# Two block products by seven: the second matrix of an MLP for two token blocks, with its weights' sums made late, and an identity matrix made on another engine

## The chip, the cores and the metric

The kernel runs on one NeuronCore of a Trainium2 chip. The core has TensorE (matrix products into PSUM), VectorE (DVE), ScalarE (ACT) and GpSimd (POOL) for elementwise work, and SyncE (SP), which here issues all DMAs from a single queue in program order. The metric is the time on the device of one execution in microseconds (us); lower is better. 0.2% of it is about what a measurement can tell.

## The reference

Three parts follow each other: an attention without a score matrix, and two MLPs. All tensors are float32 except the weights, which are float64.

```python
# q, k, v: (8 batches, 8 heads, 576, 64)
q_s = softmax(q, axis=-1);  k_s = softmax(k, axis=2)
kv = einsum('bhsd,bhse->bhde', k_s, v)
x = einsum('bhsd,bhde->bhse', q_s, kv)          # -> (4608 tokens, 512)
h = x @ w_in                                    # 512 -> 2048, the first MLP
g = maximum(h, 0) ** 2
x2 = g @ w_out                                  # 2048 -> 512: the matrix of this change
out = (sigmoid(x2 @ w_gate) * (x2 @ w_val)) @ w_out2   # 512 -> 1536 -> 512
```

## The kernel before

**Tiles and precision.** The 4608 tokens are nine blocks of 512 (numbers 0 to 8). Every float32 operand of a product is split into a rounded part hi and the rest lo, and `mm3` issues three matmuls for one product: hi hi, hi lo, lo hi (lines 217 to 219, which is why these three lines carry nearly all of TensorE's time). `hi_of` (ACT, line 211) rounds, `lo_of` (VectorE, line 214) subtracts.

**Seven products.** Most large products are 2 x 2 block products done by Strassen's seven products (`PRODUCTS`, in the order 1, 5, 6, 2, 7, 3, 4) instead of eight. The data side of it is `plan_b`: sums `b_comb` (line 715) and splits `b_hi`, `b_lo` of four quarters. The result side is `plan_seven`: three pairs of PSUM banks, with copies `e_copy` and additions `e_add` (line 777) between products. The weight side is `plan_w`: a weight group of four tiles (float64 words turned to float32 by `w_abs`, `w_low`, `w_bits`, `w_round`) is combined (`w_comb`, line 292) and split, and each hi/lo pair is stored to DRAM by `w_store` (line 296) and fetched again for every use by `w_fetch` (line 301). For the kind "out", w_out, `plan_w` stores just the four plain quarters 1, 2, 0, 4 of each group and stops.

**Stages.** Blocks 0 and 1 go through `conv_stage` while the weights are prepared. The others go in pairs (2,3), (4,5), (6,7) and the single 8 through `in_stage` (the first MLP) and `gate_stage` (the second). The order is in_stage 1, in_stage 2, gate_stage 0, gate_stage 1, in_stage 3, in_stage 4, gate_stage 2, 3, 4; the attention of later blocks runs beside them. An `in_stage` does two halves h. A half first makes 1024 columns of h and g in two units of seven products (`plan_in`), then multiplies by w_out with `o_mm`: plain 2 x 2 blocks, for two token halves tq, four kk, two output halves oh, 12 matmuls each. `o_ev` evacuates: for h = 0 a copy, stored to DRAM as "xp" (line 924); for h = 1 "xp" is loaded again (`o_ld`, line 917), added to the bank (line 913) and stored as "x2".

**Order.** All of this is added to a `Plan` with a due time and the engines' assumed durations. `Plan.trace` simulates the engines once, when the program is built: each engine takes the ready operation with the smallest due time for which buffers are free. The order so found is the program order of each engine on the chip. Buffers that matter here (`SIZES`): "W" 10 (weight tiles of 0.5 MB, fetched or to be stored), "S" 6 (split data of the second matrix), "a" 6 (results to be stored), "w" 5 (float32 weight tiles; some gate results also lie in them). Weight fetches are chained in their order of use.

**Start.** Before the plan, line 1249 calls `make_identity`: GpSimd clears `ident` and runs an affine select on it (masks.py lines 197, 199). VectorE copies `ident` with swapped columns into `swap` (line 1253), GpSimd fills `ones`, `kv` and `vt`. `ident` is used for TensorE's transposes (`k_turn`, line 404; `q_turn_pe`) and `k_put`. The first attention steps are `k_max` (lines 396 to 399), `k_turn`, and `k_mm`, the product of k^T and v (line 445).

Of the kernel before, what the change touches and what calls it, by code (L numbers as in the profile page):

```python
# [10 lines left out]
F32 = mybir.dt.float32  # L11
# [5 lines left out]
ALU = mybir.AluOpType  # L17
# [9 lines left out]
CHOSEN = object()  # L27
# [110 lines left out]
PRODUCTS = (1, 5, 6, 2, 7, 3, 4)  # L138
# [5 lines left out]
def attention_mlp_mlp(  # L144
# [159 lines left out]
    def plan_w(kind, g, T, dT, tag, conv, lead=6.0):  # L304
# [50 lines left out]
        split(3, 1, t1 + 6 * s, [M("S4")], give=[tag])  # L355
        add(t1 + 7 * s, {FREE: 0.0}, ("wfree", kind, g), lambda: None, after=[O(5), O(6), O(3)], give=[tag] * 2)


# [446 lines left out]

    def plan_seven(uid, t, nb, n, pe, tags):

# [9 lines left out]
        for i in PRODUCTS:  # L817
# [5 lines left out]
            if copy:  # L823
                for b in range(nb):
                    add(t, {ACT: ua}, E(copy, b), e_copy, uid, copy, pr, b, n, tags[copy][b], after=[names[b]], take=[tags[copy][b]])
                last[pr] = [E(copy, b) for b in range(nb)]
            elif adds:
                for b in range(nb):
                    add(t, {DVE: uv}, E(adds + "+", b), e_add, uid, adds, pr, b, n, after=[names[b], E(adds, b)])
                last[pr] = [E(adds + "+", b) for b in range(nb)]  # L830
                end[adds] = [E(adds + "+", b) for b in range(nb)]
            else:
                end["p4"] = names
# [58 lines left out]
    def o_mm(uses, gn, tq, oh, kk, pr, n):  # L892

        for m in range(2):
            ps = banks[pr[m]][:, 0:n]
            for r in range(2):
# [3 lines left out]
                mm3(ps, w[:, 0, c:c + 128], w[:, 1, c:c + 128], x[:, 0], x[:, 1], kk == 0 and r == 0, kk == 3 and r == 1)  # L900

    def o_ev(key, bank, h, n, engine):
        src = banks[bank][:, 0:n]
# [11 lines left out]
    def o_ld(key, c):  # L915
        t = tile2("a", "xp")[:, c]
        nc.sync.dma_start(out=t, in_=x2d["xp", key[0], key[1]][:, c])
        z_t[key] = t

    def o_st(key, h, c):  # L920
# [153 lines left out]
    BLOCKS = [(2 * n, 2 * n + 1) for n in range(NPAIR)] + [(NB - 1,)]  # L1074

    def in_stage(n, t):

# [4 lines left out]
        for h in range(2):  # L1082
            G = ("G", n, h)
            gready = defaultdict(dict)
            for u in range(2):
# [10 lines left out]
                freed[prs[0]] = (t, fin)  # L1096

            for kk in range(4):
                for qn, (name, where) in gready[kk].items():
# [138 lines left out]
    for i, (stage, n) in enumerate(STAGES):  # L1238
# [3 lines left out]
        if stage is gate_stage and n == 0:  # L1242
            preps = [("gv", g) for g in range(gv_n)] + [("out2", g) for g in range(out2_n)]
            for m, (kind, g) in enumerate(preps):
                plan_w(kind, g, T1 - 40 + (t + 40 - T1 + 40) / len(preps) * m, 10.0, "w", None)
        t = stage(n, t)

    ctx.enter_context(tc.manual_schedule())
    make_identity(nc, ident)
    nc.gpsimd.memset(ones, 1.0)  # L1250
# [73 lines left out]
```

## Time and profile before

| | us |
|---|---|
| three timed runs | 1709.07, 1710.23, 1712.56 |
| median | 1710.23 |
| the profiled execution | 1712.01 |
| its span, first to last instruction | 1709.9 |
| TensorE busy in the span | 1645.8 (96%) |
| VectorE busy | 1123.3 (66%) |
| ACT busy | 921.4 (54%) |
| GpSimd busy | 20.7 (1%) |
| DMA, share of its 16 engines' time | 74% |

Busy time counts overlapping instructions of one engine once. Matmuls overlap each other in the trace (each is shown for about 0.39 us, and one starts every 0.227 us), so a stretch in which TensorE's busy time equals its length is one in which matmuls follow each other without a gap. The span is what the program itself takes; some 2 us lie around it.

### The profile page before, as it was taken

What the parts mean: (1) busy time and instruction counts of PE and PEld (TensorE: products, weight loads), DVE (VectorE), ACT (ScalarE), POOL (GpSimd) and SP (SyncE); (2) the same over time, 40 slices, a digit from 0 to 9 for tenths busy, and PEclk for the clock granted to TensorE, in tenths of its full rate; (3) what the DMA queues carried; (4) which work ended last, traced back from release to release, by engine and by line L of the source; (5) the groups of instructions that cost most, each with busy time, mean ns of one, the idle gap of its engine ahead of it and who ended that gap; (6) DMA issues with size and microseconds to landing.
All of it is one profiled execution on the core that took longest, in us unless ns stands there. A gap on an engine that the chain in (4) does not pass through costs nothing.

```text
span 1709.9 us, 25346 instructions
## 1 busy us (share of the span) xinstructions
PE 1645.8 (96%) x9276; PEld 1412.5 (83%) x9276; DVE 1123.3 (66%) x2078; ACT 921.4 (54%) x1718; POOL 20.7 (1%) x43
## 2 busy tenths in 40 slices
PE   4898999999899999999999999999999999999999
PEld 2676777877777888889888998889998899889998
DVE  6889768888865687588366874353364594448446
ACT  5688657758463655366355645263443453335344
POOL 0000000000000000000000000000000000000000
PEclk9899999999999999999999999999999999999999
DMA  7778888888697979976766573557777567555797
GB/s 257 268 281 320 320 316 308 309 288 313 210 349 259 357 260 370 334 255 206 242 214 197 194 236 121 210 185 285 283 285 242 191 204 239 194 195 185 239 379 269
DMA packets 163484, 443.30 MB, mean 259 GB/s; under 512 B 15648, under 2 KB 45856, under 8 KB 163360
## 3 DMA queue, kind: packets, MB, share of 16 engines
q1 hardware_dynamic: 163360, 441.68, 74.0%
q8 instruction: 74, 1.21, 0.3%
q14 instruction: 50, 0.41, 0.1%
HBM read 357.20 MB, written 84.41 MB: 258 GB/s over the span
## 4 chain that ended last, share of the span: by engine, by line
PE 81%; DVE 7%; DMA 6%; ACT 4%; issue 2%; SPq 0%; POOL 0%; DVEq 0%; POOLq 0%; ACTq 0%
PE bank L217 26%; PE bank L218 26%; PE bank L219 26%; DMA w_gv<-whl 2%; PE xps L595 2%; DMA wraw<-in_moe_w_gate_dram 1%; DVE whl L214 1%; DMA ws<-w_in 1%; DVE bX L214 1%; PE kps L452 1%; DVE wf L271 1%; DVE wf L278 1%; DMA wraw<-in_moe_w_out_dram 0%; DVE wf L268 0%; ACT whl L211 0%
## 5 line engine op out<-in xcount | busy, mean ns | idle before, releaser
L217 PE MATMUL bank<-bX,ws 128*128 128x512 f32 (+1 forms) x1288 | 476.3, 370 | 7.6 <-DMA ws<-w_in 5.9
L219 PE MATMUL bank<-bX,ws 128*128 128x512 f32 (+1 forms) x1288 | 472.2, 367 | 0.0
L218 PE MATMUL bank<-bX,ws 128*128 128x512 f32 (+1 forms) x1288 | 472.2, 367 | 0.0
L777 DVE TENSOR_TENSOR s<-s,bank 128x512 f32<-128x512 f32 (+1 forms) x303 | 189.8, 633 | 221.7 <-PE bank L219 177.1
L217 PEld LDWEIGHTS bank<-bX,ws 128*128 128x128 f32 x1288 | 243.5, 189 | 48.3 <-DMA ws<-w_in 6.3
L211 ACT ACTIVATE s<-bank 128x512 f32<-128x512 f32 (+1 forms) x303 | 164.4, 553 | 212.9 <-PE bank L219 195.8
L219 PEld LDWEIGHTS bank<-bX,ws 128*128 128x128 f32 x1288 | 243.2, 189 | 40.0
L218 PEld LDWEIGHTS bank<-bX,ws 128*128 128x128 f32 x1288 | 243.5, 189 | 37.9 <-issue 0.2
L211 ACT ACTIVATE bS<-s 128x512 fp32r<-128x512 f32 (+1 forms) x306 | 175.6, 582 | 156.5 <-PE bank L219 145.3
L214 DVE TENSOR_TENSOR bS<-s,bS 128x512 fp32r<-128x512 f32 (+1 forms) x306 | 190.6, 632 | 77.4 <-ACT bS L211 72.5
L217 PE MATMUL bank<-ws,bS 128*128 128x256 f32 x756 | 214.4, 284 | 0.0
L219 PE MATMUL bank<-ws,bS 128*128 128x256 f32 x756 | 214.0, 283 | 0.0
L218 PE MATMUL bank<-ws,bS 128*128 128x256 f32 x756 | 213.9, 283 | 0.0
L217 PE MATMUL bank<-bS,ws 128*128 128x512 f32 (+1 forms) x512 | 187.9, 367 | 4.3 <-DMA ws<-w_out 3.2
L218 PE MATMUL bank<-bS,ws 128*128 128x512 f32 (+1 forms) x512 | 186.4, 364 | 0.0
L219 PE MATMUL bank<-bS,ws 128*128 128x512 f32 (+1 forms) x512 | 186.3, 364 | 0.0
L217 PEld LDWEIGHTS bank<-ws,bS 128*128 128x128 f32 x756 | 145.0, 192 | 1.0
L218 PEld LDWEIGHTS bank<-ws,bS 128*128 128x128 f32 x756 | 145.0, 192 | 0.7
L796 ACT ACTIVATE s<-s 128x512 f32<-128x512 f32 (+1 forms) x120 | 70.4, 589 | 139.1 <-DVE s L777 138.6
L219 PEld LDWEIGHTS bank<-ws,bS 128*128 128x128 f32 x756 | 145.0, 192 | 0.0
L217 PEld LDWEIGHTS bank<-bS,ws 128*128 128x128 f32 x512 | 97.1, 190 | 20.7 <-DMA ws<-w_out 3.6
L219 PEld LDWEIGHTS bank<-bS,ws 128*128 128x128 f32 x512 | 97.1, 190 | 15.3
(128 smaller groups left out, 2131.4 us busy)
## 6 DMA issues: line engine op xcount, KB each, us to landing
ws<-w_gv SPq DMA_DIRECT2D x210, 512.0 KB, 4.4
ws<-w_out SPq DMA_DIRECT2D x185, 512.0 KB, 4.4
ws<-w_in SPq DMA_DIRECT2D x128, 512.0 KB, 6.0
w_gv<-whl SPq DMA_DIRECT2D x42, 512.0 KB, 5.2
w_out<-whl SPq DMA_DIRECT2D x37, 512.0 KB, 4.9
w_in<-whl SPq DMA_DIRECT2D x32, 512.0 KB, 4.1
wraw<-in_moe_w_out_dram SPq DMA_DIRECT2D x28, 512.0 KB, 5.5
vt<-in_v_dram SPq DMA_DIRECT2D x32, 325.0 KB, 5.9
```

What stands on the lines that cost most here:

```text
L211: nc.scalar.activation(out=dst, in_=src, func=AF.Copy)
L214: by_name[engine].tensor_tensor(out=dst, in0=src, in1=hi.bitcast(F32), op=ALU.subtract)
L217: nc.tensor.matmul(ps, ah, bh, start=first, stop=False, skip_group_check=True)
L218: nc.tensor.matmul(ps, ah, bl, start=False, stop=False, skip_group_check=True)
L219: nc.tensor.matmul(ps, al, bh, start=False, stop=last, skip_group_check=True)
L271: nc.vector.scalar_tensor_tensor(out=w, in0=high, scalar=-0x40000000, in1=w, op0=ALU.bitwise_and, op1=ALU.bitwise_or)
L278: by_name[engine].tensor_tensor(out=w, in0=w, in1=low, op=ALU.add)
L452: nc.tensor.matmul(ps[rows, o:o + D + 1], kt[:, r, rows], vt[:, r, c:c + D + 1], start=(r == 0), stop=(r == RK - 1), skip_group_check=True,)
L595: nc.tensor.matmul(ps[:, e], kvf[b % 2][p], t[:, e], start=True, stop=True)
L777: nc.vector.tensor_tensor(out=t, in0=t, in1=banks[pr[b]][:, 0:n], op=ALU.add)
L796: nc.scalar.activation(out=t, in_=t, func=AF.Sigmoid)
```

## The change

The second matrix of the first MLP is done by seven products for blocks 6 and 7 (`SEVEN`, both halves of `in_stage` 3). `seven_out` takes the place of the plain loop there: `plan_b` forms and splits the sums of g, `p_o1` issues 6 matmuls for each of the seven products, each kk and each of two banks, `plan_seven` evacuates. For h = 1 the copies become additions to the "xp" tile that was loaded (`e_old`). `o_st1` stores.

Seven products need the weights' four sums. `plan_out_sums` makes them, for each of the four groups: it loads the four stored pairs again (`w_again`), adds hi and lo to a whole tile (`w_whole`), forms S1 to S4 (`w_comb`), splits and stores them as products 5, 7, 6, 3. It is due around the end of the first gate stage, the groups 16 us apart, each after the one before.

The identity is made by VectorE: a row of column numbers by doubling, its transpose in blocks of 32, and a comparison for each of the four blocks on the diagonal. The fills of `ones`, `kv` and `vt` stay on GpSimd.

```diff
+    def w_again(g, b, i):
+        t = tile4("W", "wa")
+        nc.sync.dma_start(out=t.bitcast(F32), in_=wd["out", g, i])
+        wraw["out", g, b] = t
+    def w_whole(g, b):
+        t, hl = tile2("w", "wf"), wraw.pop(("out", g, b)).bitcast(F32)
+        nc.vector.tensor_tensor(out=t, in0=hl[:, 0], in1=hl[:, 1], op=ALU.add)
+        wf["out", g, b] = t
+    def plan_out_sums(g, T, dT, wait):
+        V = lambda b: ("vs", g, b)
+        M = lambda nm: ("wm", "out", g, nm)
+        O = lambda i: ("wo", "out", g, i)
+        for b, i in enumerate((1, 2, 0, 4)):
+            add(T + b * dT - 6, {DMA: 1.5}, ("vl", g, b), w_again, g, b, i, after=[("ws", "out", g, i), *wait], take=["W"])
+            add(T + b * dT, VEC, V(b), w_whole, g, b, after=[("vl", g, b)], take=["w"], give=["W"])
+        T += 4 * dT
+        for nm, o, a, b, op, after, i in (
+            ("S1", 3, 2, 3, ALU.add, [V(2), V(3)], 5), ("S3", 2, 0, 2, ALU.subtract, [V(0), M("S1")], 7),
+            ("S2", 0, 3, 0, ALU.subtract, [M("S3"), M("S1")], 6), ("S4", 1, 1, 0, ALU.subtract, [M("S2"), V(1)], 3),
+        ):
+            key = ("out", g, i)
+            add(T, VEC, M(nm), w_comb, "out", g, o, a, b, op, CHOSEN, after=after)
+            add(T + 0.2, {ACT: 0.63}, ("wh",) + key, w_hi, key, o, "W", after=[M(nm)], take=["W"])
+            add(T + 0.4, LOW, ("wo",) + key, w_lo, key, o, CHOSEN, after=[("wh",) + key])
+            add(T - 10, {DMA: 1.5}, ("ws",) + key, w_store, key, after=[O(i)], give=["W"])
+            T += dT
+        add(T, {FREE: 0.0}, ("wfree", "out", g, 1), lambda: None, after=[O(5), O(7), M("S2"), O(6), O(3)], give=["w"] * 4)
...
+    def e_old(uid, nm, pr, b, n, key):
+        t = z_t.pop(key)
+        nc.vector.tensor_tensor(out=t, in0=t, in1=banks[pr[b]][:, 0:n], op=ALU.add)
+        ev[uid, nm, b] = t
...
+                    if old:
+                        key = old(copy, b)
+                        add(t, {DVE: uv}, E(copy, b), e_old, uid, copy, pr, b, n, key, after=[names[b], ("old",) + key])
+                        continue
...
+    def p_o1(use, gn, i, kk, pr, n):
+        w = whl[use]
+        x = bs[gn + (kk,), i]
+        for m in range(2):
+            c = 256 * (kk % 2) + 128 * m
+            mm3(banks[pr[m]][:, 0:n], w[:, 0, c:c + 128], w[:, 1, c:c + 128], x[:, 0], x[:, 1], i in OPENS and kk == 0, kk == 3)
...
+    def o_st1(where, key, h, c):
+        z_t[key] = ev.pop(where)
+        o_st(key, h, c)
...
+    SEVEN = {(3, 0), (3, 1)}
+    def seven_out(n, h, t, js, nt, mm, G, gready):
+        per = 24 * mm * SLOW
+        for kk in range(4):
+            nm = G + (kk,)
+            for qn, (name, where) in gready[kk].items():
+                def bind(nm=nm, qn=qn, where=where):
+                    bq.setdefault(nm, {})[qn] = ev.pop(where)
+                add(t - 8, {FREE: 0.0}, ("bind", nm, qn), bind, after=[name])
+            times = {i: t + per * x + per / 4 * kk - 6 for x, i in enumerate(PRODUCTS)}
+            quarters = ("11", "12", "21", "22")
+            plan_b(nm, {qn: [("bind", nm, qn)] for qn in quarters}, times, "S", nt, {qn: ["f"] for qn in quarters})
+        sorder.extend([("bhi", G + (kk,), i) for i in PRODUCTS for kk in range(4)])
+        uid = ("o1", n, h)
+        def place(nm, b):
+            oh, tq = {"s1": (0, 0), "s2": (0, 1), "s5": (1, 1), "p4": (1, 0)}[nm]
+            if len(js) > 1:
+                return (js[tq], 2 * oh + b), slice(0, N)
+            return (js[0], 2 * oh + b, tq), slice(nt * tq, nt * tq + nt)
+        names = (("s1", 1), ("s5", 5), ("s2", 6), ("p4", 4))
+        if h:
+            for nm, i in names:
+                for b in range(2):
+                    key, c = place(nm, b)
+                    add(
+                        t + per * PRODUCTS.index(i) - 6, {DMA: 0.8}, ("old",) + key, o_ld, key, c,
+                        after=[("ost",) + key[:2] + (0,) + key[2:], ("blo", G + (0,), i)], take=["a"],
+                    )
+        def pe(i, pr, t, wait):
+            for kk in range(4):
+                use = (uid, i, kk // 2)
+                if kk % 2 == 0:
+                    plan_fetch(("out", 2 * h + kk // 2, i), use, t - 14)
+                nm = ("p", uid, i, kk)
+                add(
+                    t, {PE: 6 * mm}, nm, p_o1, use, G, i, kk, pr, nt,
+                    after=[("wf", use), ("blo", G + (kk,), i)] + (wait if kk == 0 else [("p", uid, i, kk - 1)]),
+                    give=["S"] + (["W"] if kk % 2 else []),
+                )
+                t += 6 * mm * SLOW
+            return [nm] * 2, t
+        end, prs, t = plan_seven(
+            uid, t, 2, nt, pe, {x: ["a", "a"] for x in ("s1", "s5", "s2")}, (lambda nm, b: place(nm, b)[0]) if h else None
+        )
+        fin = []
+        for b in range(2):
+            e = ("e", uid, "p4", b)
+            if h:
+                key = place("p4", b)[0]
+                add(t, {DVE: 0.7}, e, e_old, uid, "p4", prs[0], b, nt, key, after=[end["p4"][b], ("old",) + key])
+            else:
+                add(t, {ACT: 0.6, DVE: 0.7}, e, z_copy, uid, prs[0], b, nt, "a", CHOSEN, after=[end["p4"][b]], take=["a"])
+            fin.append(e)
+            for nm, _ in names:
+                key, c = place(nm, b)
+                last = e if nm == "p4" else end[nm][b]
+                add(t - 4, {DMA: 0.8}, ("ost",) + key[:2] + (h,) + key[2:], o_st1, (uid, nm, b), key, h, c, after=[last], give=["a"])
+        freed[prs[0]] = (t, fin)
+        return t
...
+            if (n, h) in SEVEN:
+                t = seven_out(n, h, t, js, nt, mm, G, gready)
+                continue
...
+            for g in range(NU):
+                wait = [("wfree", "out", g - 1, 1)] if g else [("wfree",) + x for x in preps]
+                plan_out_sums(g, t + D2_ - 10 + 16 * g, 2.0, wait)
...
-    make_identity(nc, ident)
+    col, row = (cst.tile([128, 32], F32, name=x) for x in ("colnum", "rownum"))
+    nc.vector.memset(col[:, 0:1], 0.0)
+    nc.vector.memset(col[:, 1:2], 1.0)
+    for n in (2, 4, 8, 16):
+        nc.vector.tensor_scalar(out=col[:, n:2 * n], in0=col[:, 0:n], scalar1=float(n), scalar2=None, op0=ALU.add)
+    nc.vector.memset(ident, 0.0)
+    nc.vector.transpose(out=row, in_=col)
+    for i in range(4):
+        c = slice(32 * i, 32 * i + 32)
+        nc.vector.tensor_tensor(out=ident[c, c], in0=row[c], in1=col[c], op=ALU.is_equal)
```

## Rows read from the trace of the kernel before

**Rows 1.** The page: busy us, share of the span and instructions of each engine.

```profile
PE 1645.8 (96%) x9276; PEld 1412.5 (83%) x9276; DVE 1123.3 (66%) x2078; ACT 921.4 (54%) x1718; POOL 20.7 (1%) x43
```

**Rows 2.** Busy time by stretch: us, each engine's (instructions), PEclk granted, DMA share, GB/s.

```profile
25.00:150.00 125.00, 103.09 (x454) 76.83 (x454) 112.90 (x236) 99.51 (x213) 0.00 (x0) 0.88 0.82 299
...
330.00:660.00 330.00, 316.40 (x1460) 258.62 (x1458) 240.21 (x428) 194.61 (x348) 3.82 (x5) 0.98 0.83 295
660.00:795.00 135.00, 134.78 (x751) 117.67 (x752) 98.67 (x162) 70.75 (x117) 1.41 (x2) 1.00 0.82 289
795.00:875.00 80.00, 80.00 (x486) 69.95 (x485) 43.95 (x79) 37.00 (x60) 2.41 (x3) 1.00 0.71 230
...
947.00:1013.00 66.00, 66.00 (x536) 64.06 (x535) 59.66 (x101) 38.59 (x66) 0.00 (x0) 1.00 0.65 206
...
1049.00:1094.50 45.50, 45.50 (x200) 37.03 (x199) 12.94 (x22) 11.71 (x20) 0.00 (x0) 1.00 0.27 94
1094.50:1134.70 40.20, 40.20 (x177) 32.69 (x176) 23.72 (x45) 26.43 (x48) 0.00 (x0) 1.00 0.73 259
1134.70:1178.30 43.60, 43.60 (x194) 36.08 (x194) 16.11 (x30) 10.88 (x23) 0.00 (x0) 1.00 0.51 177
1178.30:1198.40 20.10, 20.10 (x169) 20.10 (x168) 9.29 (x24) 12.79 (x35) 0.00 (x0) 1.00 1.00 389
```

**Rows 3.** Who TensorE waited for, whole span: total us, times, longest.

```profile
PE bank L404 <- DVE kmx L399: 14.5, 2, 12.6
...
PE bank L217 <- DMA ws<-w_in: 5.9, 1, 5.9
...
PE bank L217 <- DMA ws<-w_out: 3.2, 1, 3.2
...
PE bank L217 <- DMA ws<-w_gv: 0.7, 1, 0.7
```

**Rows 4.** Busy time of instructions on tile bS alone, second matrix of h = 1.

```profile
1134.80:1178.20 43.40, 43.40 (x192) 35.80 (x191) 7.50 (x11) 6.94 (x11) 1.00 0.51 176
```

**Rows 5.** Timeline of VectorE: start, us, what; two operations in a row.

```profile
170.69 1.29 DVE L292 TENSOR_TENSOR wf<-wf 128x512 f32<-128x512 f32 x2
```

**Rows 6.** Who the DMA queue waited for, whole span.

```profile
SPq L296 <- DVE whl L214: 140.6, 55, 7.3
```

**Rows 7.** Timeline of the start; then kt, vt, wraw: first and last issue, landing.

```profile
10.01 0.28 POOL masks.py:199 TENSOR_SCALAR_AFFINE_SELECT ident<-ident 128x128 f32<-128x128 f32 x1 [9.08 <-issue]
...
10.32 1.44 DVE L1253 COPY swap<-ident 128x64 f32<-128x64 f32 x2 [10.32 <-POOL ident masks.py:199]
...
10.53 1.23 DVE L396 TENSOR_TENSOR kmx<-kt 128x256 f32<-128x256 f32 x1
...
18.22 2.36 PE L445 MATMUL bank<-vt,kt 128*128 128x129 f32 x10
...
18.67 0.16 DVE L559 TENSOR_SCALAR qst<-qst 128x8 f32<-128x8 f32 x1
...
23.64 0.66 ACT L254 ACTIVATE wf<-wraw 128x512 f32<-128x512 f32 x1
...
L377 SPq DMA_DIRECT2D kt<-in_k_dram x1: 399/399/399, 0.7 to 0.7; - x1
...
DMA to landing us min/median/max: 3.1/3.1/3.1
...
L383 SPq DMA_DIRECT2D vt<-in_v_dram x1: 860/860/860, 4.9 to 4.9; - x1
...
DMA to landing us min/median/max: 6.5/6.5/6.5
...
L244 SPq DMA_DIRECT2D wraw<-in_moe_w_in_dram x2: 327/328/328, 8.5 to 9.1; - x2
...
DMA to landing us min/median/max: 6.6/6.9/7.2
```

**Rows 8.** The reductions on GpSimd: ns min/median/max, first and last start.

```profile
L422 POOL PARTITION_ALL_REDUCE kgm<-kmx x24: 704/705/1001, 161.3 to 922.1; - x24
```

More of the change, by code (lines that the diff above doesn't have):

```diff
@@ L8 @@
 from concourse._compat import with_exitstack
-from concourse.masks import make_identity
 F32 = mybir.dt.float32
@@ L804, in e_mul, with plan_seven @@
         by_name[engine].tensor_tensor(out=t, in0=t, in1=ev.pop((uid, o, b)), op=ALU.mult)
-    def plan_seven(uid, t, nb, n, pe, tags):
+    def e_old(uid, nm, pr, b, n, key):
+        t = z_t.pop(key)
+        nc.vector.tensor_tensor(out=t, in0=t, in1=banks[pr[b]][:, 0:n], op=ALU.add)
+        ev[uid, nm, b] = t
+    def plan_seven(uid, t, nb, n, pe, tags, old=None):
         order = sorted(pairs, key=lambda x: freed[x][0] if freed[x] else -1)
```

## The prediction

> **What bounds the kernel now.** I read the page's busy lines first: TensorE is busy for 1645.8 us of a span of 1709.9 us, so the other engines can only matter through it [rows 1]. Then the busy times by stretch, to see where the missing 64 us lie. The reader is to see two different kernels in that table [rows 2]. From 25 to 150 us TensorE works 103.1 of 125 us and VectorE 112.9: the prologue, a chain through VectorE. From 660 us on TensorE's busy time equals the stretch to within 0.2 us in every row, and VectorE's is anything from 36% to 90% of it: there the number of matmuls sets the time. The list of what TensorE waited for agrees [rows 3]: one wait of 12.6 us for VectorE's first maxima (14.5 us in two), and two for weight tiles (5.9 and 3.2 us). The change touches one thing in each of these two regimes, so I cost them apart.
>
> **Part 1, fewer matmuls in the second matrix of blocks 6 and 7.** Removed: each half h of that stage issues 2 tq x 4 kk x 2 oh x 12 = 192 matmuls of 128x512; the seven products need 7 x 4 x 6 = 168. For h = 1 the 192 took 43.40 us without a gap [rows 4], so 0.226 us each, and the clock is already at its upper level (1.00 granted, 2.4 GHz) [rows 2]. Two halves lose 48 matmuls: 48 x 0.226 = 10.85 us. As TensorE is continuous there, all of it counts, unless something that is added is late.
>
> **What is added beside these matmuls.** Each half now splits 28 operands where it split 16 (ACT rounds, VectorE subtracts), forms 16 differences on VectorE, and evacuates 14 banks where it evacuated 8. For h = 1 VectorE gains 12 + 16 + 6 = 34 operations. Two in a row take 1.29 us [rows 5], 0.69 for the first and 0.60 for each further one, so 34 take 20.5 us. VectorE was busy 16.1 of 43.6 us in that stretch [rows 2]; it would be 36.6 of 38.0 us, 96%. For h = 0 (12.9 us now) the same sum gives 33.4 us. The nearest stretch with products of this form ran VectorE at 59.7 of 66 us, 90%, and TensorE lost nothing [rows 2]; 96% is beyond it. What eases it: the stretches before and behind have VectorE at 23.7 of 40.2 and 9.3 of 20.1 us, and about 6 of 28 splits can run ahead into the six S buffers. What speaks against it: a product is 24 x 0.226 = 5.4 us, and its bank pair is wanted again two products later, so VectorE may run one product late and no more. Bounds: 0, and, if nothing at all could be shifted and each operation took its full 0.69 us, 16.1 + 34 x 0.69 - 38.0 = 1.6 us for h = 1, with as much again if the lateness recurs at the stage behind (block 8 waits for its own splits in the same VectorE queue). I take 1 us. ACT's 12 extra roundings per half (about 7 us) fit: ACT is busy 11 to 12 of 44 us in these stretches [rows 2]. The 12 extra fetches of weights (0.5 MB each) come where DMA moves 94 and 177 GB/s [rows 2], at one per 2.7 us, the rate at which the stretch 1094.5 to 1134.7 already fetches: nothing. The loads and stores of partial sums are as many as before.
>
> **The weights' sums.** For each of four groups: 4 loads of a stored hi/lo pair, 4 additions, 4 combinations, 4 ACT roundings, 4 subtractions, 4 stores. That is 48 VectorE operations, 48 x 0.60 = 29 us, 16 on ACT, and 32 transfers of 0.524 MB = 16.8 MB. The code makes them due at the start of the gate stage of blocks 2 and 3, near 800 us, and runs the groups one behind the other, 16 us apart. In 795 to 875 us VectorE is busy 43.95 of 80 us: with 29 more it is at 73, which the 90% stretch covers. DMA moves 230 GB/s there, 18.4 MB; with 16.8 more 440 GB/s would be wanted, more than the 389 GB/s of the busiest row [rows 2]. So the sums take longer than planned, about 35.2 / 0.389 = 90 us, which is harmless in itself: the first product that reads them is near 1055 us. It is not harmless that every load and store stands in SP's one queue. A store waits there for VectorE's subtraction (140.6 us of such waits in this trace, the longest 7.3 [rows 6]), and every weight fetch behind it waits too; so does one behind a load that waits for a free W buffer. The same mixture, the other weights being prepared, stands in 660 to 795 us, and TensorE lost 0.2 us of 135; in 330 to 660 us it stands beside two large waits for weights (5.9 and 3.2 us [rows 3]). Bounds: 0, and one wait of 5.9 us per group, 23.6 us. Nearest in kind (a gate stage, fetches of w_gv) is 660 to 795, so I take 1 us.
>
> **Part 2, the identity on VectorE.** Now GpSimd waits 9.08 us before its select, which ends at 10.3; VectorE then makes swap (1.44 us) and starts the first maximum at 10.53, slowed to 1.23 us beside GpSimd's fills; the first k^T v product starts at 18.22 [rows 7]. The first K tile had landed at 0.7 + 3.1 = 3.8 us. Removed: that wait. Added: 12 small VectorE operations in front of swap. Small ones take 0.16 us [rows 7]; at 0.2 each with swap's 1.44 they end near 0.7 + 2.4 + 1.4 = 4.5. Between the first maximum and 18.22 lie 7.7 us, or 6.9 if that maximum takes some 0.4 us, so the product could start at 11.4; its V tile lands at 4.9 + 6.5 = 11.4 too. Gain 18.22 - 11.4 = 6.8 us at most. At the other end, 12 operations at a full 0.69 us and swap end at 10.4 and leave about 0.8 us of gain. I take 6.5, by the small rows. Next in line is the first weight tile, which ACT took up at 23.64 and which lands by 9.1 + 7.2 = 16.3: not late for 17.1. The gain reaches the end if the prologue moves as a whole: its transfers are released by buffers that its own steps free, and it draws 299 GB/s of the 389 seen elsewhere [rows 2].
>
> The row shows GpSimd idle for 9.08 us with no instruction in it. The Trainium skill, page "GPSIMD Engine Reference", section 2.1 Instruction dispatch, says that the first call of a freshly loaded kernel pays a load of about 6 us that no profile instruction shows. By that figure, an estimate, part 2 would give 6 instead of 6.5 us and the time would be 0.5 us longer; the measured 9.08 decides. The rule also means that GpSimd's next user, the reduction over partitions, might pay at its first call what the select no longer pays; its first call here took 0.96 us against a median of 0.705 [rows 8], so this trace does not show such a payment, and it has 150 us to happen unseen.
>
> **Sum.** -10.85 - 6.5 + 1 + 1 = -15.35 us. The profiled execution took 1712.0 us (2.1 around its span), 1.8 over the median of the three runs, 1710.2. So 1696.7 for an execution like the profiled one, and 1694.9 for the median: 1695.
>
> **Rivals.** (A) The prologue gives nothing back: what part 2 wins is taken by the waits for weights behind it (5.9 and 3.2 us), if these hang on DMA's own pace and not on the kernel's steps. Against it: DMA is not full there (295 GB/s over 330 to 660 us [rows 2]). Then -10.85 + 2 = -8.85: 1701.4. (B) VectorE becomes the bound in the two seven-product stretches: both halves and the stage behind run late by 1.6 us each, about 5 us, and the sums cost one 5.9 us wait: -10.85 - 6.5 + 5 + 5.9 = -6.5: 1703.8. For it: 96%. Against it: the 90% stretch without loss. (C) Slower: each of the four groups of sums blocks SP once as long as the worst wait, because four loads and four pending stores can hold 8 of the 10 W buffers and leave fetches two tiles (5.4 us) ahead: 4 x 5.9 = 23.6 us, -17.35 + 23.6 = +6.3: 1716.5. It decides from 17.35 us of stalls on, that is from four waits of 4.3 us. Against it: TensorE's waits for w_gv in the whole trace are one, of 0.7 us [rows 3], under the other preparations too. (D) The seven products don't come about for half of the work, or the first fetches wait for sums: as the sums have 170 us to spare, I give it nothing of its own.
>
> **How the numbers follow.** Forecast 0.70, A 0.12, B 0.11, C 0.07. The lowest time I can work out is -10.85 - 6.8 with no cost at all: 1692.6, less about 1 us for the spread of the medians, so low is 1691.5. The range reaches over A and to B: high 1704. That leaves out C and some of B. A measurement here tells 0.2% (3.4 us) from no change: the line for faster is 1706.8. Faster: forecast, A and most of B, 0.89. Same, between 1706.8 and 1713.6: 0.05 (the rest of B, a mild C). Slower: 0.06.
>
> **What would show it.** Right: the first maximum starts between 4 and 5 us and the first k^T v product near 11.5; the two stretches of `bank<-bS,ws` hold 168 matmuls each and take about 38 us; the stretch with the sums still has TensorE at its full length. Wrong: a wait for `ws<-w_gv` between 795 and 900 us in TensorE's list (C), a wait for ACT or VectorE's bS, or for an evacuation, near 1050 to 1180 (B), or a prologue that starts 6.5 us earlier and reaches 660 us as late as before (A).

## The result, and the profile after

The changed kernel takes **1692.51 us** (median of four runs, 1689.85 to 1693.58) against 1711.22 (1709.07 to 1712.56, four runs): ratio 0.9889, 95% interval 0.9874 to 0.9905, or 18.7 us less (16.3 to 21.6). The forecast, 1695, is 2.5 us above it, and the range held it. The profiled execution took 1693.58 us, its span 1691.8. Line numbers of the kernel after: `mm3` L216 to L218, `hi_of` L210, `lo_of` L213, `e_add` L807, `w_whole` L364, `k_max` L426 to L429, `k_turn` L434, `k_mm` L475.

The page's busy line, where [rows 1] had 9276 matmuls:

```profile
PE 1637.9 (97%) x9228; PEld 1405.4 (83%) x9228; DVE 1189.2 (70%) x2201; ACT 951.2 (56%) x1767; POOL 20.3 (1%) x41
```

Busy time by stretch (columns as in [rows 2]). The stretches with the sums (787 to 867) and with the second matrix of blocks 6 and 7 (1042 to 1087.9 and 1122.5 to 1163.6) answer to 795 to 875, 1049 to 1094.5 and 1134.7 to 1178.3 there:

```profile
25.00:150.00 125.00, 102.97 (x466) 77.28 (x467) 111.64 (x229) 98.42 (x214) 0.00 (x0) 0.89 0.82 299
330.00:660.00 330.00, 319.51 (x1468) 261.49 (x1467) 240.34 (x427) 195.80 (x350) 3.81 (x5) 0.98 0.84 299
660.00:787.00 127.00, 127.00 (x718) 111.25 (x718) 93.07 (x153) 67.17 (x111) 1.41 (x2) 1.00 0.81 281
787.00:867.00 80.00, 79.10 (x479) 68.82 (x478) 59.99 (x105) 38.42 (x66) 1.70 (x2) 1.00 0.91 325
867.00:940.00 73.00, 73.00 (x391) 59.24 (x390) 58.08 (x111) 50.65 (x75) 3.12 (x4) 1.00 0.89 330
940.00:1006.00 66.00, 66.00 (x536) 64.11 (x535) 59.71 (x102) 38.68 (x66) 0.00 (x0) 1.00 0.67 206
1042.00:1087.90 45.90, 45.90 (x203) 37.30 (x202) 31.97 (x55) 24.44 (x42) 0.00 (x0) 1.00 0.62 208
1122.50:1163.60 41.10, 41.10 (x194) 34.45 (x193) 32.38 (x56) 19.17 (x36) 0.00 (x0) 1.00 0.80 269
```

The matmuls on tile bS alone in those last two ([rows 4]):

```profile
1042.00:1087.90 45.90, 40.43 (x168) 31.25 (x168) 16.11 (x25) 13.43 (x22) 1.00 0.62 208
1122.40:1163.60 41.20, 38.90 (x168) 31.16 (x168) 15.61 (x23) 14.43 (x23) 1.00 0.80 269
```

Who TensorE waited for ([rows 3]):

```profile
PE bank L434 <- DVE kmx L429: 7.4, 2, 4.8
...
PE bank L216 <- DMA ws<-w_in: 4.6, 1, 4.6
...
PE bank L216 <- DMA ws<-w_out: 2.6, 1, 2.6
```

GpSimd's first reduction, from its timeline:

```profile
155.60 0.98 POOL L452 PARTITION_ALL_REDUCE kgm<-kmx  x1 [152.93 <-DVE kmx L429]
```

The start on the timeline ([rows 7]):

```profile
0.92 1.09 DVE L1378 TENSOR_SCALAR colnum<-colnum 128x2 f32<-128x2 f32 x4
...
2.29 0.77 DVE L1383 TENSOR_TENSOR ident<-rownum,colnum 32x32 f32<-32x32 f32 x4
...
3.10 0.30 DVE L1387 COPY swap<-ident 128x64 f32<-128x64 f32 x2
...
3.63 0.42 DVE L426 TENSOR_TENSOR kmx<-kt 128x256 f32<-128x256 f32 x1 [0.23 <-DMA kt<-in_k_dram]
...
4.76 0.48 PE L434 MATMUL bank<-ident,kmx 128*128 128x128 f32 x1 [4.76 <-DVE kmx L429]
...
10.96 2.49 PE L475 MATMUL bank<-vt,kt 128*128 128x129 f32 x10 [0.90 <-ACT kmx L445]
```

Three things are to be seen. TensorE is still without a gap from 660 us on, but for 0.9 us in the sums' stretch. The half that was 192 matmuls is 168. And the first maximum starts at 3.63 us instead of 10.53, the first k^T v product at 10.96 instead of 18.22.

**Where the time went.** The start of the same matmul in a trace minus its start in the trace of before, in us, at the places named by their time in before. "Sums" lies between the columns 758 and 947, the two seven-product halves between 1043, 1100 and 1198. From 1198 to the end nothing more happens, but in e7 and e9, where block 8 is changed too: e7 ends at -22.6, e9 at -21.7.

| trace | 12.6 | 34 | 146 | 345 | 600 | 758 | 947 | 1043 | 1100 | 1198 |
|---|---|---|---|---|---|---|---|---|---|---|
| after | -7.8 | -5.6 | -5.5 | -5.7 | -8.2 | -8.0 | -6.9 | -6.9 | -12.2 | -17.6 |
| e11, after again | -7.8 | -8.2 | -6.9 | -3.9 | -9.4 | -9.3 | -8.1 | -8.1 | -13.4 | -18.8 |
| e1, identity only | -8.0 | -7.6 | -7.5 | -7.9 | -14.1 | -13.9 | -13.9 | -13.9 | -13.9 | -13.9 |
| e2, seven only | +0.5 | +2.1 | +2.0 | +1.1 | -0.9 | +1.1 | +2.0 | +2.0 | -3.3 | -8.7 |
| e3, sums unused | -7.4 | -5.3 | -5.1 | -5.6 | -9.4 | -8.7 | -7.0 | -7.0 | -7.0 | -7.0 |
| e4, no sums | -7.9 | -7.1 | -7.0 | -7.6 | -10.0 | -9.8 | -9.8 | -9.8 | -15.0 | -20.5 |
| e5, select beside | -7.3 | -5.1 | -5.1 | -5.6 | -7.3 | -6.5 | -5.0 | -5.0 | -10.3 | -15.8 |
| e6, identity late | -3.5 | -3.1 | -3.2 | -3.6 | -7.7 | -6.2 | -5.1 | -5.1 | -10.4 | -15.8 |
| e7, block 8 too | -7.7 | -6.8 | -6.7 | -6.5 | -13.6 | -13.4 | -13.1 | -13.1 | -18.4 | -23.8 |
| e9, half of block 8 | -7.8 | -6.9 | -6.9 | -6.6 | -11.4 | -10.6 | -9.3 | -9.3 | -14.6 | -20.0 |
| e10, VectorE dose | -8.0 | -7.6 | -7.1 | -7.7 | -12.8 | -12.2 | -10.5 | -10.5 | -11.5 | -10.1 |
| e8, before again | +0.5 | -0.6 | +0.8 | +3.1 | +1.2 | +3.1 | +3.1 | +3.1 | +3.1 | +3.1 |
| e12, before again | +0.4 | +0.1 | +0.3 | -0.3 | -3.6 | -2.9 | -2.9 | -2.9 | -2.9 | -2.9 |

Up to the place 758 every engine has the same order of work in all these traces, but for the start; the first operation that the change adds there is a load of a stored pair, at 800 us in after.

### The profile page after: what moved, and what is told of

Read it like the earlier page. It is cut to its first block, busy times and chain, and to the rows that moved or that the text cites. A ratio compares the mean times of both kernels' runs of the same rounds, so it can differ in the third digit from the quotient of the medians.

```text
span 1691.8 us, 25550 instructions
## 1 busy us (share of the span) xinstructions
PE 1637.9 (97%) x9228; PEld 1405.4 (83%) x9228; DVE 1189.2 (70%) x2201; ACT 951.2 (56%) x1767; POOL 20.3 (1%) x41
## 4 chain that ended last, share of the span: by engine, by line
PE 80%; DVE 7%; DMA 7%; ACT 4%; issue 1%; SPq 0%; DVEq 0%; ACTq 0%
PE bank L216 26%; PE bank L217 26%; PE bank L218 26%; DMA w_gv<-whl 2%; PE xps L625 2%; DMA wraw<-in_moe_w_gate_dram 1%; DVE whl L213 1%; DVE bX L213 1%; DMA ws<-w_in 1%; PE kps L482 1%; DVE wf L270 1%; ACT whl L210 1%; DVE wf L277 1%; DMA wraw<-in_moe_w_out_dram 1%; ACT wf L253 0%
## 5 line engine op out<-in xcount | busy, mean ns | idle before, releaser
L216 PE MATMUL bank<-bX,ws 128*128 128x512 f32 (+1 forms) x1288 | 477.0, 370 | 7.6 <-DMA ws<-w_in 4.6
L218 PE MATMUL bank<-bX,ws 128*128 128x512 f32 (+1 forms) x1288 | 472.7, 367 | 0.0
L807 DVE TENSOR_TENSOR s<-s,bank 128x512 f32<-128x512 f32 (+1 forms) x309 | 192.8, 633 | 208.6 <-PE bank L218 169.0
L210 ACT ACTIVATE s<-bank 128x512 f32<-128x512 f32 (+1 forms) x309 | 168.1, 554 | 214.9 <-PE bank L218 213.5
L216 PEld LDWEIGHTS bank<-bX,ws 128*128 128x128 f32 x1288 | 243.7, 189 | 48.8 <-DMA ws<-w_in 5.0
L218 PEld LDWEIGHTS bank<-bX,ws 128*128 128x128 f32 x1288 | 243.6, 189 | 40.3
L210 ACT ACTIVATE bS<-s 128x512 fp32r<-128x512 f32 (+1 forms) x322 | 185.1, 584 | 135.0 <-PE bank L218 122.1
L213 DVE TENSOR_TENSOR bS<-s,bS 128x512 fp32r<-128x512 f32 (+1 forms) x322 | 201.0, 633 | 54.6 <-ACT bS L210 49.1
L216 PE MATMUL bank<-ws,bS 128*128 128x256 f32 x756 | 214.5, 284 | 0.0
L218 PE MATMUL bank<-ws,bS 128*128 128x256 f32 x756 | 214.0, 283 | 0.0
L216 PE MATMUL bank<-bS,ws 128*128 128x512 f32 (+1 forms) x496 | 182.4, 368 | 2.6 <-DMA ws<-w_out 2.6
L217 PE MATMUL bank<-bS,ws 128*128 128x512 f32 (+1 forms) x496 | 180.0, 363 | 0.0
L218 PE MATMUL bank<-bS,ws 128*128 128x512 f32 (+1 forms) x496 | 180.0, 363 | 0.0
L216 PEld LDWEIGHTS bank<-ws,bS 128*128 128x128 f32 x756 | 144.9, 192 | 1.0
L218 PEld LDWEIGHTS bank<-ws,bS 128*128 128x128 f32 x756 | 144.8, 192 | 0.0
L210 ACT ACTIVATE whl<-wf 128x512 fp32r<-128x512 f32 x127 | 78.4, 626 | 70.6 <-PE bank L218 21.6
L216 PEld LDWEIGHTS bank<-bS,ws 128*128 128x128 f32 x496 | 94.0, 190 | 18.2 <-DMA ws<-w_out 3.1
```

Source lines behind the costliest of these rows:

```text
L210: nc.scalar.activation(out=dst, in_=src, func=AF.Copy)
L213: by_name[engine].tensor_tensor(out=dst, in0=src, in1=hi.bitcast(F32), op=ALU.subtract)
L216: nc.tensor.matmul(ps, ah, bh, start=first, stop=False, skip_group_check=True)
L217: nc.tensor.matmul(ps, ah, bl, start=False, stop=False, skip_group_check=True)
L218: nc.tensor.matmul(ps, al, bh, start=False, stop=last, skip_group_check=True)
L807: nc.vector.tensor_tensor(out=t, in0=t, in1=banks[pr[b]][:, 0:n], op=ALU.add)
```

## The experiments

The theory: the forecast's four terms, with nothing of the early start given back. The rivals: A (the waits for weights take it back), B (VectorE bounds the seven-product stretches), C (the sums block SP). After the first runs a further one, V: the sum's remainder is a difference between executions, in the waits for weights before 660 us.

**e1: the identity alone.** The `make_identity` line of the kernel before is replaced:

```diff
-    make_identity(nc, ident)
+    (the VectorE lines of the change, colnum to is_equal)
```

> The kernel before with the identity made by VectorE and nothing else. Theory P (the parts add up): the first transpose 7.8 us earlier, the prologue settled at -5.7 us by 100 us, and that, with what the waits for weights between 340 and 560 us give, arrives at the end: -6 to -8 us, 1703 to 1705. Rival A (the later waits for weights take the gain): within 2 us of before, at the earliest by 560 us.

Measured: 1701.01 us (1696.07 to 1703.77) against 1711.69; ratio 0.9938 (0.9917 to 0.9960), -10.7 us. That is less than the 1703 to 1705 expected. The trace stands at -7.5 to -8.0 up to 345 us and at -13.9 from 758 us on: rival A's sign is the wrong way round. Nothing is taken back; 6 us more come in between 345 and 600 us, where no line of code differs. The profiled execution is one of the faster ones (1697.78 us), so its 6 us are no measure of the median.

**e2: the seven products alone**, with the identity on GpSimd as before:

```diff
-    (the VectorE lines of the change, colnum to is_equal)
+    make_identity(nc, ident)
```

> The changed kernel with the identity made by GpSimd as before. P: 48 matmuls of 0.2267 us less is -10.9, the sums +1.2, so -9.5 to -10.5 us: 1700 to 1702. The waits for weights near 466 and 529 us stay at about 5.9 and 3.2 us if they follow the start; if they vary from run to run, they differ here too, although nothing ahead of 740 us is changed. Rival (the early start also makes room for the sums): the stretch of the sums loses more than 1.2 us of TensorE here.

Measured: 1701.16 us (1699.33 to 1706.27), ratio 0.9942 (0.9924 to 0.9960), -10.5 us. That is in the range expected, 1700 to 1702. In its trace the two halves give -5.3 and -5.4, the sums cost 0.9.

**e3: the sums made, nothing multiplied with them.**

```diff
-    SEVEN = {(3, 0), (3, 1)}
+    SEVEN = set()
```

> The changed kernel in which the sums are made and stored but blocks 6 and 7 are multiplied by plain blocks, so the sums are read by nothing. P: what the identity gives less the sums' 1.2 us: 1.2 us slower than the kernel with the identity alone, 1704 to 1706, and TensorE's one wait in the stretch of the sums (0.9 us behind an evacuation by ACT) comes again. Rival (the sums cost nothing, that wait is chance): equal to the identity alone.

Measured: 1703.95 us (1701.03 to 1707.02), ratio 0.9956 (0.9939 to 0.9973), -7.7 us. The trace loses 1.75 us between 758 and 947; the seven products alone are then the rest of after's 18.7, 11.0 us (10.7 in after's trace).

**e4: the seven products without the sums.** The four sums' fetches take a stored plain quarter each, and `plan_out_sums` isn't called: the making of the sums is left out, the 336 matmuls of the two halves are as in after:

```diff
-    plan_fetch(("out", 2 * h + kk // 2, i), use, t - 14)
+    plan_fetch(("out", 2 * h + kk // 2, {5: 0, 6: 1, 7: 2, 3: 4}.get(i, i)), use, t - 14)
...
-    plan_out_sums(g, t + D2_ - 10 + 16 * g, 2.0, wait)
```

> The changed kernel without the sums: their loads, additions, combinations, splits and stores are left out, and products 5, 6, 7 and 3 fetch the four plain quarters in their place, so the same work is done on wrong weights. P: 1.2 us faster than the changed kernel, 1691, and the two seven-product stretches lose 10.7 us against before as they do with the sums. Rival (later costs of the sums, in W buffers or in the late attention): 3 us or more faster than the changed kernel.

Measured: 1691.19 us (1686.82 to 1692.09), ratio 0.9876 (0.9855 to 0.9896), -20.5 us. The trace has exactly no change from 758 to 1043 us, so the 1.2 us of after are the sums'. Its two stretches with TensorE, VectorE and DMA as in [rows 2]:

```profile
787.00:867.00 80.00, 80.00 (x479) 69.63 (x478) 43.09 (x78) 35.96 (x57) 2.41 (x3) 1.00 0.70 233
867.00:940.00 73.00, 73.00 (x402) 59.54 (x400) 48.18 (x93) 41.08 (x64) 2.42 (x3) 1.00 0.63 208
```

Against after, the sums add 16.9 us of VectorE and 92 GB/s in the first stretch and 9.9 us and 122 GB/s in the second.

Where the 1.2 us are is seen in after's waits of all engines from 800 to 830 us (total us, times, longest):

```profile
DVE wf L364 <- DMA wa<-w_out: 7.2, 4, 3.7
...
ACT whl L210 <- DMA w_out<-whl: 1.8, 1, 1.8
...
PE bank L216 <- ACT p L210: 0.9, 1, 0.9
```

and in its timeline of TensorE:

```profile
822.22 0.39 PE L218 MATMUL bank<-bX,ws 128*128 128x512 f32 x1
823.50 0.50 PE L216 MATMUL bank<-bX,ws 128*128 128x512 f32 x1 [0.90 <-ACT p L210]
```

ACT's rounding of a sum (`whl`) waits 1.8 us for a W buffer that is held until an earlier sum's store has landed (`w_out<-whl`). Behind it in ACT's queue stands the evacuation `p` that frees a bank, and TensorE waits 0.9 us for that; the two matmuls start 1.28 us apart, where 0.23 is usual, which is nearly all of the 1.2. The same wait (0.6 to 1.5 us) stands in all other traces with sums but e7, which lost only 0.3 us there (e2, e3, e5, e6, e9, e10, e11), and in none without (the three of before, e1, e4); a wait of TensorE for w_gv in these stretches stands in none. So the price is paid through ACT's queue, not through SP's: rival C doesn't occur, and the term of 1 us was right for a reason other than the one given.

**e5: the select kept, but off the path.** GpSimd runs the affine select on another tile after its fills; VectorE makes the identity:

```diff
+    make_identity(nc, kvf[1][3])
+    nc.gpsimd.memset(kvf[1][3], 0.0)
```

> The changed kernel with GpSimd's affine select kept, behind its fills, on a tile that nothing else needs at that time. Theory W (what cost was the wait of VectorE and TensorE for the select): equal to the changed kernel, 1692 within 3 us, first maximum still near 3.6 us although the select ends near 12 us. Rival (the load of the select's code itself slows what runs beside it, DMA or VectorE): the first 30 us are 2 us or more later than in the changed kernel, and the end too.

Measured: 1692.35 us (1692.00 to 1695.44) against 1709.81, ratio 0.9903 (0.9889 to 0.9918), -17.5 us: as after. GpSimd's timeline, and the first transpose:

```profile
5.29 0.47 PE L435 MATMUL bank<-ident,kmx 128*128 128x128 f32 x1 [5.29 <-DVE kmx L430]
...
13.86 0.28 POOL masks.py:199 TENSOR_SCALAR_AFFINE_SELECT kv<-kv 128x128 f32<-128x128 f32 x1 [11.03 <-issue]
```

The select still waits, 11.03 us here, and costs nothing at the end when nobody waits for it. (The first transpose is 0.5 us later than in after.) What part 2 removes is a wait on the path and not work.

**e6: the identity made late.** VectorE first does a fill and six passes over a PSUM bank (the lines of the change are left out below):

```diff
+    nc.vector.memset(banks[5], 0.0)
+    for _ in range(6):
+        nc.vector.tensor_scalar(out=banks[5], in0=banks[5], scalar1=1.0, scalar2=None, op0=ALU.add)
     (the VectorE lines of the change)
```

> The changed kernel with a fill and six passes over a PSUM bank (128x512, about 0.6 to 0.7 us each) on VectorE ahead of the identity. Theory W, dose: the first maximum starts about 4.4 us later, near 8 us, and all of it reaches the end: 1696 to 1698. Rival (the start only passes through in part, as later waits take it up): less than 2 us at the end.

Measured: 1696.61 us (1689.91 to 1700.83), ratio 0.9923 (0.9903 to 0.9942), -13.2 us. The first transpose starts at 9.10 us, 4.3 later than in after, and the median is 4.3 us above e5's, in the 1696 to 1698 expected. Its profiled execution, though, ends where e5's does (-15.8): 1.9 us of difference are left at 34 us, and the rest is made up between 345 and 600. The medians are for the theory, the single trace is for V.

**e7, e9: more of the same.** Block 8 too, both halves (e7) or its first half alone (e9):

```diff
-    SEVEN = {(3, 0), (3, 1)}
+    SEVEN = {(3, 0), (3, 1), (4, 0), (4, 1)}     (e7)
+    SEVEN = {(3, 0), (3, 1), (4, 0)}             (e9)
```

> The changed kernel with the seven products for block 8 as well (256 columns, both halves). P: 48 matmuls of 128x256 less, 0.12 us each, is -5.8 us: 1687. Rival (VectorE becomes the bound: a product lasts only 2.9 us there, with up to 8 splits and differences of 0.42 us and two evacuations): TensorE waits for bS or for evacuations near 1185 to 1250 us and less than half of the 5.8 us arrives, 1690 or more.

> The changed kernel with the seven products for the first half of block 8 too, but not for the second, where the run with both halves lost 3.1 us and a fall of the granted clock behind a VectorE at 93%. Theory R (VectorE has room in the first half, 15 of 23 us, and has none in the second, where the splits of the next gate stage also fall): the first half gives its 24 x 0.12 = 2.9 us and no wait appears near 1185 to 1245 us: 1690 in a comparison in which the changed kernel has 1692.5. Rival (the seven products at 256 columns don't pay at all): 1692.5 or more.

Measured: e7 1694.13 us (1688.71 to 1701.62), ratio 0.9923 (0.9901 to 0.9945), -15.7 us, no better than after and not the 1687 expected (its profiled execution is its fastest); e9 1689.93 us (1684.66 to 1693.62), ratio 0.9876 (0.9857 to 0.9895), -21.0 us, the lowest ratio with e4's (which leaves the sums out) and as expected (1690), though its interval overlaps after's, so that it isn't shown to be better. Busy times of e7's two halves of block 8:

```profile
1175.00:1198.00 23.00, 23.00 (x194) 23.00 (x194) 15.05 (x42) 13.00 (x35) 0.00 (x0) 1.00 0.97 347
1219.00:1245.00 26.00, 22.02 (x143) 20.86 (x142) 24.24 (x59) 15.15 (x34) 0.00 (x0) 0.87 0.85 330
```

A wait of TensorE in e7, and one in e9:

```profile
PE bank L216 <- ACT bX L210: 4.0, 2, 2.9
...
PE bank L216 <- DMA ws<-w_out: 1.1, 2, 0.7
```

The first half is full at 15.05 of 23 us of VectorE. In the second VectorE is at 24.24 of 26 us, the next stage's operand bX comes late through it and ACT, TensorE stands for 2.9 and 1.0 us, and the granted clock of the stretch, 1.00 before it, is 0.87: a mean of the two levels of 1.2 and 2.4 GHz, as behind the first stop some 25 matmuls start 0.21 us apart instead of 0.12. That is rival B, in the stage where the operations are half as long (256 columns) and as many. In both traces the first half gives 2.9 us (24 matmuls). In e7 the second one, which was to give as much, costs 4.2; in e9, where it is plain, 1.2 us are lost there, with TensorE waiting 1.1 for weights of w_out, which that run's expectation (no wait) didn't have.

**e10: VectorE given more to do.** One pass more behind each of the 16 differences of a half, about 16 x 0.60 = 9.6 us:

```diff
         by_name[engine].tensor_tensor(out=t[o], in0=t[a], in1=t[b], op=ALU.subtract)
+        if nm[0] == "G":
+            nc.vector.tensor_tensor(out=t[o], in0=t[o], in1=t[o], op=ALU.max)
```

> The changed kernel with one more VectorE pass (128x512, 0.60 us back to back) behind each of the 16 differences of both seven-product halves: 9.6 us more per half, VectorE from 32.0 and 32.4 us to some 42 us in stretches of 46 and 41 us. Theory B' (VectorE was near its limit, as the prediction's 96% had it): TensorE waits for bS in both halves, 2 us or more each, 1697 or more. Rival S (there is slack, since splits run ahead into the neighbouring stretches, where VectorE is busy 70% or less): less than 1 us lost in all.

Measured: 1703.21 us (1697.23 to 1712.97, ten runs), ratio 0.9957 (0.9939 to 0.9975), -7.7 us, 11 worse than after. Busy times in e10, in 40 us of the first half and around the second:

```profile
1035.00:1075.00 40.00, 37.27 (x157) 28.38 (x157) 39.42 (x68) 23.84 (x43) 0.00 (x0) 1.00 0.51 171
1125.00:1170.00 45.00, 40.45 (x181) 32.88 (x180) 37.42 (x65) 17.02 (x33) 0.00 (x0) 0.96 0.65 219
1135.00:1140.00 5.00, 2.31 (x7) 1.56 (x6) 4.97 (x9) 1.65 (x3) 0.00 (x0) 0.76 0.61 210
```

and in after, in 40 us of each half:

```profile
1035.00:1075.00 40.00, 40.00 (x177) 32.44 (x177) 35.54 (x61) 28.27 (x50) 0.00 (x0) 1.00 0.57 194
1115.00:1155.00 40.00, 40.00 (x178) 33.11 (x177) 37.39 (x65) 24.65 (x45) 0.00 (x0) 1.00 0.73 242
```

Who TensorE waited for in e10:

```profile
PE bank L217 <- DVE bS L213: 3.6, 5, 1.2
...
PE bank L216 <- issue: 2.7, 1, 2.7
```

In the table the two halves, -5.3 and -5.4 in after, are -1.0 and +1.4 here: 4.3 and 6.8 us dearer, for 9.6 us of VectorE each. Theory B' holds, its rival of a slack for 9.6 us doesn't. After's shares of 70% and 79% (31.97 of 45.90 and 32.38 of 41.10 us) understate how full VectorE was: at the end of each half it has little left to do, and in the 40 us shown it is busy 89% and 93%, with TensorE gapless. In e10 it is busy 99% of the same 40 us of the first half, and TensorE stands for 2.7 of them. In the second half not all of the 6.8 us is VectorE's doing alone: the stop of 2.7 us, for which the profile names no releaser, is followed by a fall of the granted clock (0.76 over 1135 to 1140 us, part of it at the lower level of 1.2 GHz). The added pass also lengthens the chain from a difference to its matmuls; that is not separated from VectorE's load, for which the 99% speaks. The share isn't a limit by itself, though: e7's second half lost at 93% of 26 us, where after lost nothing at 93% of 40.

**e8, e11, e12: the same kernels again**, for V; no edit.

> The kernel before, unchanged, for a second trace of it. Theory V (the waits for weights near 466 and 529 us, and TensorE's clock in the first 45 us, differ between executions of one program): the two waits are not 5.9 and 3.2 us again but 1 us or more off in sum, and the start of the products at 43 us may move by 2 us with the clock. Rival F (they belong to the program): 5.9 and 3.2 us and 43.05 us again within 0.3 us, so that what the changed kernel won between 340 and 560 us is its own doing.

> The changed kernel, unchanged, for a second trace. Theory V (waits and clock differ between executions): the start of the products (37.4 us), the two waits for weights (4.6 and 2.6 us) and the wait in the stretch of the sums (0.9 us) each move by up to 2 us, while the two seven-product stretches lose 10.7 us against before again within 0.3 us. Rival F: all of them repeat within 0.3 us.

> The kernel before, for a third trace of it. The time that it needs from 390 to 640 us is 1.8 us less than in the first trace in the second one, and 1.8 to 7 us less in the seven traces with an early start (2.1 in the one with a late start). Theory V: chance between executions, and this trace may lie as low as the early ones (3 us or more below the first). Theory E (an early start makes these waits shorter): 0 to 2.1 us below the first.

Measured: e8 1715.1, e11 1692.36, e12 1709.14 us. The table shows three traces of before ending 6 us apart (+3.1, 0, -2.9) and two of after 1.2 apart. The differences arise up to 345 us and between 345 and 758. e12 has the 3 us that V asked for between 390 and 640 us (3.3). In e11 the halves repeat (10.7) and the start of the products moves (37.4 to 35.7 us), as V had it. e8's two waits for weights repeat more closely than V had it (5.8 and 2.8 us for 5.9 and 3.2), and yet the trace moves by several us.

Between 345 and 758 us, two of the steps can be named. One is a wait of TensorE in before:

```profile
PE bank L217 <- DVE xp L913: 1.1, 1, 1.1
```

It stands in before, e8 (1.3) and e2 (0.9), and not in e12, e1 and both of after, which gain 1.4 us there. The other is the clock behind the wait for w_out, in before and at nearly the same matmuls in e12:

```profile
534.00:536.00 2.00, 2.00 (x6) 1.52 (x6) 0.09 (x1) 0.81 (x2) 0.00 (x0) 0.50 0.48 49
...
533.00:535.00 2.00, 2.00 (x11) 1.65 (x10) 0.58 (x2) 1.31 (x3) 0.00 (x0) 1.00 0.52 88
```

TensorE had waited 3.2 us in before and 2.8 in e12; then the grant was 0.50 (1.2 GHz) in the one and 1.00 in the other, 1.6 us. e8 and e11 have those 1.6 us too, after (which had waited 2.6) doesn't. Both steps come and go between executions of one program. The wait for w_in's weights in e12:

```profile
PE bank L217 <- DMA ws<-w_in: 5.7, 1, 5.7
```

The same in e6:

```profile
PE bank L216 <- DMA ws<-w_in: 3.2, 1, 3.2
```

It is 5.7, 5.8 and 5.9 us in the three traces of before, 4.3 in e2 with its late start, 4.6 and 4.1 in the two of after, and 2.8 (e7) to 5.3 (e4) in the other traces with VectorE's identity.

## Why the prediction was right, and where not

**Fewer matmuls: right.** 48 matmuls were to give 10.85 us; the two halves gave 5.28 + 5.44 = 10.72 in after and as much in e2, e4, e5, e6 and e11.

**VectorE beside them: the term of 1 us was mis-sized; it is 10.85 - 10.72 = 0.13.** The step of the sum that failed is the 96%: all 34 operations were charged to 38 us. Measured are 32.4 of 41.1 us (79%) for h = 1 and 32.0 of 45.9 (70%) for h = 0. Matmuls of neighbouring units stand between those of bS (194 matmuls in the h = 1 stretch, 168 of them on bS), so the stretches are longer than the 38 us forecast (40.8 and 45.6 from the first matmul on bS to the last), and only 23 and 25 of VectorE's operations on bS lie in them; the others lie outside. The 90% stretch as a sign of cover came true (89% and 93% of 40 us, nothing lost), but e7 shows that a share alone is no proof: it lost at 93%. The prediction's lowest share of VectorE, 36%, is misread: the row from 1049 us has 12.94 of 45.5, 28%; nothing hangs on it. Rival B was a real mechanism, at most 10 us of VectorE per half away.

**The sums: 1.2 us measured (1.24 in e11, 0.3 in e7 to 1.75 in e3 in the other traces), 1 forecast; their place was wrong.** VectorE was at 60.0 of 80 us, not 73, since the sums stretched over both stretches: in 867 to 940 it is still 9.9 us above e4. That the sums take some 90 us was right: their loads start at 800.0 and the last store of a pair at 891.8 us. DMA reached 325 and 330 GB/s. The stall came through ACT's queue, which it hadn't followed: of the added steps' queues the prediction follows SP's only.

**The identity: right in kind.** The first maximum came at 3.63 us, before the 4 to 5 forecast; the twelve operations ended at 3.1 us as estimated, and swap took 0.30 us, not 1.44; the first k^T v product started at 10.96 us (forecast 11.4). That is 7.3 us at this point, more than the 6.8 "at most": V's tile, which was to bound it at 11.4, was issued earlier too (4.5 us) and landed near 10.8. At 345 us, of the traces with the early identity, 3.9 to 7.9 are left. The forecast's 6.5 lies in the middle, and that it fits one trace (5.7 in after) or another (6.5 in e7) is partly luck, as the last section shows.

The select's wait of 9.08 us [rows 7] and 11.03 us in e5 had no instruction in it. The Trainium skill, page "GPSIMD Engine Reference", section 2.1 Instruction dispatch, gives some 6 us for a load at a first call; both rows are longer, so the measurement decides. By its rule the first reduction might have paid instead; it took 0.98 us in after, and 0.96 in before, and doesn't show it.

Swap's copies, 1.44 us for two while GpSimd filled `kv` [rows 7], took 0.30 us with the fills over. The Trainium skill, page "SBUF — State Buffer", section Who interferes with whom, says that copies of VectorE can contend with GpSimd for a shared pair of ports; the rows agree. By it an operation with two inputs doesn't contend with a fill, which only writes, and yet the first maximum took 1.23 us beside them and 0.42 without; as its row starts at 10.53 us, while swap's copies ran (10.32 to 11.76), it may have waited for these. No run separates the two.

**What the sum lacked.** Its terms, as measured in after's trace, are -5.7 (345 us) + 1.2 - 10.7 = -15.2, the forecast. The remaining -2.3 us come between 345 and 758 us, where the code is the same, and no term stands for them. 1.4 of them are the wait for VectorE's `xp`, which e12 lacks as well, with its late start: a difference between executions. 1.3 are the shorter wait for w_in's weights, and the rest nearly cancels. So the forecast's closeness to the median, 2.5 us, is in part luck. Over all traces those with VectorE's identity gain 0.9 to 7.0 us there on the first trace of before, 3.8 in the mean of ten; of the other three, e2 and e8 gain nothing and e12 2.6. So a part may be an effect of the early start on the waits for weights, rival A with its sign turned; for it speaks that w_in's wait is never below 5.7 us in the three traces of before, against it that it is no longer in e2 (4.3 us, late) than in e1 (4.4, early). This stays open.

## What to carry to other kernels

Where TensorE runs without gaps, count matmuls: the saving came out to within 0.13 us. When operations are added beside them, don't add their time to the stretch that names them, but ask how far they can run ahead, and follow every queue that they stand in (here ACT's) for what is behind them. A wait at the very start of a chain can be worth most of its length if what follows is released by the chain itself (here 9.08 us of wait, 7.8 at the first transpose, 3.9 to 7.9 later), and a repeated trace of the unchanged kernel tells how much of a remainder needs no cause at all.

## What was not expected of the hardware

Ten k^T v products ran at two paces. The second group on TensorE's timeline in before:

```profile
24.05 1.28 PE L445 MATMUL bank<-vt,kt 128*128 128x129 f32 x10
```

in after, with two pairs of other products:

```profile
16.03 2.05 PE L625 MATMUL xps<-qf,kv 128*128 128x512 f32 x2 [1.29 <-ACT kv L499]
17.87 1.89 PE L475 MATMUL bank<-vt,kt 128*128 128x129 f32 x10
...
22.63 2.05 PE L625 MATMUL xps<-qf,kv 128*128 128x512 f32 x2 [0.69 <-issue]
```

and in e11, the same program:

```profile
16.01 1.10 PE L625 MATMUL xps<-qf,kv 128*128 128x512 f32 x2 [1.29 <-ACT kv L499]
16.94 1.28 PE L475 MATMUL bank<-vt,kt 128*128 128x129 f32 x10
```

Busy times and the granted clock (PEclk) at these places, in after and then in e11:

```profile
17.00:20.00 3.00, 2.87 (x13) 2.10 (x11) 0.38 (x4) 1.86 (x4) 0.00 (x0) 1.00 0.43 158
22.60:24.40 1.80, 1.77 (x2) 0.79 (x3) 1.70 (x7) 1.12 (x2) 0.00 (x0) 0.50 0.99 377
...
16.00:18.00 2.00, 1.99 (x12) 1.52 (x13) 1.19 (x4) 1.98 (x4) 0.00 (x0) 1.00 0.92 346
```

One program needed 1.89 us for the group in one execution and 1.28 in the other. The clock explains it, but after's 1.00 from 17 to 20 us has to be read with care: its trace holds no record of the granted clock before 19.13 us, and without a record the view prints 1.00. Matmul by matmul, the group's first six start 0.20 to 0.22 us apart and the others, from 19.15 us on, 0.11. The slow pace is that of the lower level (1.2 GHz): the pair of `xps` takes 2.05 us at 16.03, ahead of the records, and 2.05 again at 22.63, where a grant of 0.50 is recorded, against 1.10 in e11 at a recorded 1.00. In e11 the records begin at 15.09 us, in before at 21.65. TensorE did the same work in both traces of the changed kernel up to 14.7 us, at the same times within 0.03 us, so why the clock rose 4 us later in after no row shows.

It goes with the prologue's gain. Of some 7.3 to 8.0 us at the first transpose, the three traces in which the records begin at 19.1 to 20.0 us (after, e3, e5) kept 5.1 to 5.6 at 34 us, and the six in which they begin at 14.3 to 15.1 (e1, e4, e7, e9, e10, e11) 6.8 to 8.2. So some 1 to 3 us of what the early start gives go with the time at which the clock rises, and that differs between executions of one program.
